# Attention feeding a gated MLP: token batches of 576 instead of chunks of 512, and weights that are loaded once and joined to float32 with a Prelu

## The chip, the cores and the metric

The kernel runs on one core of a Trainium2 chip. Its engines work in parallel, each on a queue of its own: TensorE (PE in the profile, its weight loads PEld), VectorE (DVE), ScalarE (ACT), GpSimd (POOL), and SyncE (SP), which issues the DMAs. The metric is the device time of one execution in microseconds (us), the median of several runs; lower is better.

## What is computed

Shapes: q, k, v are 8 batches x 8 heads x 576 tokens x 64, float32. The attention's output, as 4608 tokens of 512 numbers, is the input of a gated MLP of width 1536. The MLP's weights are 64-bit floats in memory.

```python
# two attentions, added; scale = 1/8, factor = 4
q_d, k_d, v_d = means of q, k, v over groups of 4 tokens          # 144 rows
out_up    = repeat(softmax(scale * q_d @ k_d.T) @ v_d, 4 rows each)
scores    = where(abs(i - j) < 4, scale * q @ k.T, -1e9)
out_local = softmax(scores) @ v
x = (out_up + out_local).transpose(0, 2, 1, 3).reshape(4608, 512)
# the gated MLP
gate = 1 / (1 + exp(-(x @ w_gate)))                               # 512 -> 1536
val  = x @ w_val
out  = (gate * val) @ w_out                                       # 1536 -> 512
```

## The kernel before

**Attention** comes in 32 units: a unit is one batch and one pair of heads (unit u is batch u // 4, pair u % 4). A unit is written as some 13 steps (`unit_steps`): sums of 4 tokens on POOL (`sum4`, L384/L386), local scores (s, L465), maximum, subtraction and exponential (L476 to L478), sums and division (L483 to L487), the downsampled scores and their softmax (sd, e; L508 to L528), transposes (at, adt), v, and last `av_local` (x), which multiplies with v, adds the downsampled part (od) and writes a quarter of the contraction rows of a token tile `xT`, as a high and a low float16 half (L594/L596).

**The MLP** takes tokens in 9 chunks of 512 (CH). Every product of the MLP is made of float16 halves in three matmuls (high x high, high x low, low x high; `product`, L391 to L395). For one of 12 slices of the width (fc) `moe_gate` issues 4 x 3 matmuls of 512 columns, then ScalarE takes the tanh (L622); `moe_val` does the same with w_val, then VectorE multiplies (L630), ScalarE writes the high half g (L638) and VectorE the low half (L639); `moe_out` adds that slice's share to four accumulators o0 to o3, 4 x 3 matmuls. Gate, val and the four accumulators have one bank of PSUM each (ps_o), the attention two (ps_a). A chunk crosses batches, so the scales of tanh and of the evictions come in up to two segments.

**The weights** are 36 pieces (12 each of gate g, val v, out o), 128 x 512 of 64-bit words, 512 KB each. All of them are loaded twice, through five stage buffers. In the first pass ("m") VectorE takes the absolute maximum of the high words (`wmax`, L153), and scales, powers of two, are made of the maxima by `wscale` (one transpose and one matmul each time). In the second pass ("c") `wconv` makes float32 of the 64-bit words: ScalarE scales the high words (L206), VectorE shifts them (L207), joins the low words by an or (L208), and puts the sign in (L209); then a gate or val piece is split by ScalarE (high, L215) and POOL (low, L216), an out piece by ScalarE and VectorE (`split`, L157/L158).

**The order** of the work is written by hand: a table T of positions, `wpos`, `gpos`, `opos`, `base` and `offset`, puts units, weight steps and the 12 slices of chunk 0 in one list up to position C1 = 56; from chunk 1 on the program writes gate, val and the former slice's out, with unit steps between them (`run_steps`). All engines take their queues in that order, as a scheduler inside the compiler places it. Chunk 1 needs tokens of batches 0 and 1, so units 0 to 7 stand ahead of it. Dummy matmuls (`awake`) stand between the first units' steps.

```python
a = raw.tile([P, WPC], I32, tag="wa", name=f"wr{k}{i}", bufs=3)
nc.scalar.activation(h.bitcast(F32), h.bitcast(F32), AF.Copy, scale=hc[:, j : j + 1])
nc.vector.tensor_scalar(out=a, in0=h, scalar1=3, scalar2=None, op0=ALU.logical_shift_left)
nc.vector.scalar_tensor_tensor(out=a, in0=l, scalar=29, in1=a, op0=ALU.logical_shift_right, op1=ALU.bitwise_or)
nc.vector.scalar_tensor_tensor(out=a, in0=h, scalar=SIGNBIT, in1=a, op0=ALU.bitwise_and, op1=ALU.bitwise_or)
```

Of the kernel before, what the change touches and what calls it, by code (L numbers as in the profile page):

```python
# [35 lines left out]
NCHUNK = NT // CH  # L36
NFC = DFF // P
# [7 lines left out]
NWT = 1 + 2 * NPC  # L45
NST = 5
# [12 lines left out]
def attention_moe(ctx, tc, qk, qkd, v, vd, wg, wv, wo, mask, out):  # L59
# [71 lines left out]
    names = {}  # L134

    def uniq(k):
        names[k] = names.get(k, 0) + 1
        return f"{k}{names[k]}"

    def pow2(dst, src):  # L140
# [22 lines left out]
    pw = cp.tile([P, NWT], F32, tag="pw", name="pw")  # L170
# [15 lines left out]
    def wmax(t, o):  # L186
        absmax(o, t[:, :, 1].bitcast(F32))
# [676 lines left out]
```

## Time and profile before

| | us |
|---|---|
| median of 3 runs | 1111.18 (1107.99 to 1111.2) |
| the profiled execution | 1110.07 |
| its span in the trace | 1108.3 |
| PE busy | 1062.2 (96%) |
| DVE busy | 547.4 (49%) |
| ACT busy | 444.1 (40%) |
| POOL busy | 364.6 (33%) |

The span runs from the first to the last instruction that the profiler recorded. PE's busy time contains the dummy matmuls and the time in which a slow clock stretches a matmul, so it is no measure of useful work by itself. An engine's share over the whole span mixes stages: about the first fifth of the span converts weights and computes the first two batches' attention, the rest is the steady sequence of gate, val and out.

### The profile page before, as it was taken

What the parts mean: (1) busy time and instruction counts of PE and PEld (TensorE: products, weight loads), DVE (VectorE), ACT (ScalarE), POOL (GpSimd) and SP (SyncE); (2) the same over time, 40 slices, a digit from 0 to 9 for tenths busy, and PEclk for the clock granted to TensorE, in tenths of its full rate; (3) what the DMA queues carried; (4) which work ended last, traced back from release to release, by engine and by line L of the source; (5) the groups of instructions that cost most, each with busy time, mean ns of one, the idle gap of its engine ahead of it and who ended that gap; (6) DMA issues with size and microseconds to landing.
All of it is one profiled execution on the core that took longest, in us unless ns stands there. A gap on an engine that the chain in (4) does not pass through costs nothing.

```text
span 1108.3 us, 17149 instructions
## 1 busy us (share of the span) xinstructions
PE 1062.2 (96%) x6831; PEld 554.8 (50%) x6831; DVE 547.4 (49%) x1038; ACT 444.1 (40%) x1048; POOL 364.6 (33%) x426
## 2 busy tenths in 40 slices
PE   8768878999998999999999999999999999999998
PEld 6543434655554555555555555555555544444443
DVE  5779989763445444444444444444444422212112
ACT  5535656443444443444334443444344422112112
POOL 8535755332433443333333443333332200000000
PEclk9859988999999999999999999999999999999999
DMA  9987866331213222232212221321120000000001
GB/s 361 382 313 262 275 211 210 110 118 59 70 56 136 70 71 70 71 109 71 70 57 101 74 80 59 109 71 59 59 97 1 2 1 38 1 1 38 1 1 38
DMA packets 31903, 110.38 MB, mean 100 GB/s; under 512 B 3536, under 2 KB 3664, under 8 KB 31824
## 3 DMA queue, kind: packets, MB, share of 16 engines
q1 hardware_dynamic: 31824, 109.30, 29.0%
q8 instruction: 54, 0.88, 0.3%
q14 instruction: 25, 0.20, 0.1%
HBM read 99.84 MB, written 9.44 MB: 99 GB/s over the span
## 4 chain that ended last, share of the span: by engine, by line
PE 86%; DVE 7%; POOL 2%; DMA 2%; ACT 2%; issue 1%; SPq 0%; DVEq 0%; POOLq 0%
PE po L395 25%; PE pv L395 24%; PE pg L395 23%; PE s L395 3%; PE x L395 3%; PE sd L395 3%; PE od L395 2%; PE at L543 2%; PE adt L553 1%; DMA qkd<-in_qkd_dram 1%; DVE hmx L153 1%; DVE wrv L209 1%; DVE wrg L208 1%; POOL kdblk L386 1%; DMA wg6c<-in_wg_dram 0%
## 5 line engine op out<-in xcount | busy, mean ns | idle before, releaser
L395 PE MATMUL pg<-xT,wg 128*128 128x512 f16 x1296 | 312.5, 383 | 11.2 <-ACT wg L215 7.3
L395 PE MATMUL pv<-xT,wv 128*128 128x512 f16 x1296 | 310.3, 381 | 5.3 <-DVE tanh L630 3.1
L395 PE MATMUL po<-g,wo 128*128 128x512 f16 x1188 | 281.2, 379 | 0.0
L395 PEld LDWEIGHTS <-wg 128*128 128x128 f16 x1296 | 125.3, 98 | 158.3 <-ACT wg L215 8.6
L395 PEld LDWEIGHTS <-wo 128*128 128x128 f16 x1296 | 126.4, 98 | 150.8 <-ACT wo L157 3.9
L395 PEld LDWEIGHTS <-wv 128*128 128x128 f16 x1296 | 125.6, 98 | 150.1 <-issue 6.4
L630 DVE SCALAR_TENSOR_TENSOR tanh<-tanh,pv 128x512 f32<-128x512 f32 x108 | 73.9, 684 | 210.2 <-PE pv L395 206.4
L622 ACT ACTIVATE tanh<-pg,tsc 128x512 f32<-128x512 f32 (+7 forms) x192 | 86.7, 497 | 176.4 <-PE pg L395 176.2
L638 ACT ACTIVATE g<-tanh,gs 128x512 f16<-128x512 f32 x99 | 71.4, 721 | 137.4 <-DVE tanh L630 135.6
L639 DVE SCALAR_TENSOR_TENSOR g<-tanh,gs,g 128x512 f16<-128x512 f32 x99 | 84.1, 849 | 52.9 <-ACT g L638 52.5
L477 POOL TENSOR_TENSOR t<-t,mx 128x640 f32<-128x640 f32 x32 | 43.4, 1357 | 164.0 <-DVE mx L476 160.1
L596 POOL TENSOR_TENSOR xT<-xs,xT 128x384 f16<-128x384 f32 (+7 forms) x54 | 48.5, 911 | 48.1 <-ACT xT L594 47.5
L585 DVE TENSOR_TENSOR xs<-x,od 128x464 f32<-128x464 f32 (+1 forms) x56 | 23.5, 452 | 72.3 <-PE x L395 72.3
L487 POOL TENSOR_TENSOR t<-t,sm 128x640 f32<-128x640 f32 x28 | 36.1, 1290 | 68.9 <-DVE sm L485 61.3
L465 DVE SCALAR_TENSOR_TENSOR t<-s,mk 128x384 f32<-128x384 f32 x64 | 30.8, 485 | 54.8 <-PE s L395 54.7
L157 ACT ACTIVATE vblk<-v,svb 64x640 f16<-64x640 f32 x48 | 39.6, 825 | 34.3 <-PE x L395 33.6
L395 PEld LDWEIGHTS s<-qk 64*64 64x64 f32 x1200 | 41.0, 138 | 21.5 <-issue 16.3
L158 DVE SCALAR_TENSOR_TENSOR vblk<-v,svb,vblk 64x640 f16<-64x640 f32 x48 | 47.9, 998 | 3.8 <-ACT vblk L157 1.7
L395 PE MATMUL s<-qk 64*64 64x64 f32 x1200 | 48.9, 227 | 0.6 <-ACT adt L535 0.6
L528 POOL TENSOR_TENSOR ad<-e,sme 72x288 f32<-72x288 f32 x52 | 37.1, 733 | 35.2 <-DVE sme L519 34.8
L511 ACT ACTIVATE e<-sd,mxd 72x144 f32<-72x144 f32 x128 | 47.1, 371 | 2.8
L384 POOL TENSOR_TENSOR qkd<-qkd 128x576 f32<-128x576 f32 x29 | 35.0, 1208 | 37.6 <-DMA qkd<-in_qkd_dram 36.9
(295 smaller groups left out, 1105.1 us busy)
## 6 DMA issues: line engine op xcount, KB each, us to landing
qk<-in_qk_dram SPq DMA_DIRECT2D x30, 610.0 KB, 3.9
qkd<-in_qkd_dram SPq DMA_DIRECT2D x29, 576.0 KB, 3.7
vd<-in_vd_dram SPq DMA_DIRECT2D x29, 384.0 KB, 3.1
v<-in_v_dram SPq DMA_DIRECT2D x32, 320.0 KB, 3.0
out_dram<-osb SPq DMA_DIRECT2D x16, 512.0 KB, 2.6
wo<-in_qk_dram SPq DMA_DIRECT2D x2, 610.0 KB, 9.9
wo<-in_qkd_dram SPq DMA_DIRECT2D x2, 576.0 KB, 9.5
out_dram<-osb SPq DMA_DIRECT2D x4, 256.0 KB, 2.4
```

Of the source, the lines that this page charges most:

```text
L157: nc.scalar.activation(hi, src, AF.Copy, scale=sc)
L158: nc.vector.scalar_tensor_tensor(out=lo, in0=src, scalar=sc, in1=hi, op0=ALU.mult, op1=ALU.subtract)
L395: nc.tensor.matmul(o, w[a], x[c], start=first and i == 0, stop=last and i == len(pairs) - 1)
L477: nc.gpsimd.tensor_tensor(out=t, in0=t, in1=mx.unsqueeze(2).to_broadcast([P, NBLK, WIN]), op=ALU.subtract)
L487: eng.tensor_tensor(out=t, in0=t, in1=sm.unsqueeze(2).to_broadcast([P, NBLK, WIN]), op=ALU.mult)
L511: nc.scalar.activation(s["e"][:, qb, h, :], pt[:QM, h * SD : (h + 1) * SD], AF.Exp, bias=mx[:, h : h + 1], scale=QKSCALE / 16, accum_out=s ...
L528: eng.tensor_tensor(out=AD[:, qb].rearrange("p c h k -> p h c k")[:, :, :, :KC], in0=s["e"][:, qb].rearrange("p h (c k) -> p h c k", c=NKC ...
L596: eng.tensor_tensor(out=x[:, hp, 1, o : o + n], in0=src, in1=x[:, hp, 0, o : o + n], op=ALU.subtract)
L622: nc.scalar.activation(t[:, o : o + n], pt[:, o : o + n], AF.Tanh, scale=tsc[:, b, fc : fc + 1])
L630: nc.vector.scalar_tensor_tensor(out=t, in0=t, scalar=1.0, in1=pt, op0=ALU.add, op1=ALU.mult)
L638: nc.scalar.activation(g[:, 0], t, AF.Copy, scale=gs[:, fc : fc + 1])
L639: nc.vector.scalar_tensor_tensor(out=g[:, 1], in0=t, scalar=gs[:, fc : fc + 1], in1=g[:, 0], op0=ALU.mult, op1=ALU.subtract)
```

## The change

- Tokens come by batches of 576 (8 of them) instead of chunks of 512 (9). Each gate, val or out tile is two halves of 288 columns (HN), each in a bank of its own, so a tile has two banks; gate, val, out and the dummy matmuls share one pool of two such tiles (ps_m), the attention has four banks. tanh, the product and g's halves take all 576 columns in one instruction each, with one scale per batch.
- `moe_out` no longer follows every slice: g of all 12 slices is kept (gq), and after a batch's last val four out tiles follow, 2 x 36 matmuls each.
- Each weight piece is loaded once, through four stage buffers. `wjoin` makes float32 of it at once: a Prelu on ScalarE with scale 2^-108 and alpha -2^32 leaves the sign where the shift keeps it, so the sign instruction goes; a shift and an or on VectorE follow, and the absolute maximum is taken of the joined numbers, which stay as float32 in place of the coming halves. Later, for two slices at a time (`wscale`) or for all out pieces (`oscale`), the scale is made, and `wsplit` splits: for gate and val VectorE multiplies by the scale in place (L249), ScalarE writes the high half and POOL the low half; for out ScalarE and VectorE split with the scale, as before.
- In each gate and val the contraction runs from the last quarter to the first, so the first matmul needs the batch's last unit.
- The order is a new table T; all loads are chained in the order in which they are written (`load`, `issue_after`).

VectorE, slices 3 and 4 of chunk 0, before: a stretch of its queue in the opening. wrv and wrg are the pieces in conversion, wv5c and wg5c their raw words, wo5m and wo6m out pieces in the first pass, t, s, sm, sme tiles of units.

```order
L207 TENSOR_SCALAR wrv5_1160<-wv5c_1101 128x512
L208 SCALAR_TENSOR_TENSOR wrg5_1122<-wg5c_1061,wrg5_1122 128x512
L153 TENSOR_REDUCE hmx_131<-wo5m_1103 128x1
L639 SCALAR_TENSOR_TENSOR wo16_111<-tanh_0_3_1196,gs_132,wo16_111 128x512
L518 TENSOR_SCALAR sme_5_1154<-sme_5_1154 72x4
L208 SCALAR_TENSOR_TENSOR wrv5_1160<-wv5c_1101,wrv5_1160 128x512
L153 TENSOR_REDUCE hmx_131<-wo6m_1167 128x1
L209 SCALAR_TENSOR_TENSOR wrg5_1122<-wg5c_1061,wrg5_1122 128x512
L465 SCALAR_TENSOR_TENSOR t_6_1310<-s_6_0_1297,mk_108 128x384
L519 RECIPROCAL sme_5_1154<-sme_5_1154 72x4
L209 SCALAR_TENSOR_TENSOR wrv5_1160<-wv5c_1101,wrv5_1160 128x512
```

The same engine after, at the first val of batch 0. The tiles wg16, wv16 hold the float32 in place of the halves, wg5 and wv5 are raw words, cw and ew scales.

```order
L249 TENSOR_SCALAR wg16_109<-wg16_109,cw_130 128x512
L249 TENSOR_SCALAR wv16_110<-wv16_110,cw_130 128x512
L208 TENSOR_SCALAR wg16_109<-wg5_917 128x512
L209 SCALAR_TENSOR_TENSOR wg16_109<-wg5_917,wg16_109 128x512
L159 TENSOR_REDUCE hmx_128<-wg16_109 128x1
L208 TENSOR_SCALAR wv16_110<-wv5_919 128x512
L209 SCALAR_TENSOR_TENSOR wv16_110<-wv5_919,wv16_110 128x512
L591 SCALAR_TENSOR_TENSOR tanh_0_0_847<-tanh_0_0_847,pv_0_0_868 128x576
L159 TENSOR_REDUCE hmx_128<-wv16_110 128x1
L164 SCALAR_TENSOR_TENSOR gq_112<-tanh_0_0_847,gq_112 128x576
```

A piece had three instructions (L207, L208, L209) and a maximum of another load; now it has a shift, an or and a maximum in a row, and a multiplication later (L249; four pieces in a row, of which the last two are shown).

ScalarE in the steady part, before (chunk 4, slices 4 and 5): tanh, the high half g, and steps of units 21 and 22 between them.

```order
L622 ACTIVATE tanh_4_4_6249<-pg_4_4_6236,tsc_139 128x256 x2
L535 COPY adt16_21_6017<-adt_21_6010 128x432
L509 ACTIVATE mxd_22_1_6021<-mxd_22_1_6021 72x2
L511 ACTIVATE e_22_5935,sme_22_5936<-sd_22_1_6019,mxd_22_1_6021 72x144 x2
L638 ACTIVATE g_4_4_6272<-tanh_4_4_6249,gs_132 128x512
L567 ACTIVATE od16_21_6072<-od_21_6068,sxb_138 128x144
L157 ACTIVATE vblk_124<-v22_5182,svb_137 64x10x64 x2
L594 CAST xT5_4768<-xs_21_6111 128x192
L594 CAST xT6_5849<-xs_21_6111 128x384
L622 ACTIVATE tanh_4_5_6325<-pg_4_5_6312,tsc_139 128x256 x2
L638 ACTIVATE g_4_5_6352<-tanh_4_5_6325,gs_132 128x512
```

ScalarE after (batch 3, slices 3 and 4), with steps of units 16 and 17 between.

```order
L586 ACTIVATE tanh_3_3_6064<-pg_3_3_6039,tsc_137 128x576
L532 ACTIVATE od16_16_6072<-od_16_6068,sxb_136 128x144
L163 ACTIVATE gq_112<-tanh_3_3_6064 128x576
L474 ACTIVATE mxd_17_1_6104<-mxd_17_1_6104 72x2
L163 ACTIVATE vblk_125<-v17_5548,svb_135 64x10x64 x2
L476 ACTIVATE e_17_6009,sme_17_6010<-sd_17_1_6102,mxd_17_1_6104 72x144 x2
L557 CAST xT4_6144<-xs_16_6134 128x576
L586 ACTIVATE tanh_3_4_6172<-pg_3_4_6147,tsc_137 128x576
L163 ACTIVATE gq_112<-tanh_3_4_6172 128x576
```

tanh is one instruction of 576 columns instead of two of 256, x goes to one token tile instead of two, and no out stands between a val and the next gate.

```diff
+HN = S // 2
-NST = 5
+NST = 4
-WGROUPS = [(0, 4), (4, NPC)]
+WGROUPS = [(0, 2), (2, 4), (4, 6), (6, 8), (8, 10), (10, NPC)]
+WUP = 2.0 ** 32
+WORDS = 2.0 ** -108
...
-    ps_o = ctx.enter_context(tc.tile_pool(name="ps_o", bufs=1, space=PSUM))
-    ps_a = ctx.enter_context(tc.tile_pool(name="ps_a", bufs=2, space=PSUM))
+    ps_m = ctx.enter_context(tc.tile_pool(name="ps_m", bufs=2, space=PSUM))
+    ps_a = ctx.enter_context(tc.tile_pool(name="ps_a", bufs=4, space=PSUM))
...
+    def load(dst_, src):
+
+        with tc.issue_after(last_load[0]) if last_load[0] is not None else nullcontext():
+            last_load[0] = nc.sync.dma_start(dst_, src).ins
...
+    def wjoin(k, i, after):
+
+        t = wraw.pop((k, i))
         h, l = t[:, :, 1], t[:, :, 0]
+        a = wwide(k, i).bitcast(I32)
+        nc.scalar.activation(h.bitcast(F32), h.bitcast(F32), AF.Prelu, scale=WORDS, alpha=-(2.0 ** 32))
+        with behind(after):
+            nc.vector.tensor_scalar(out=a, in0=h, scalar1=3, scalar2=None, op0=ALU.logical_shift_left)
+        nc.vector.scalar_tensor_tensor(out=a, in0=l, scalar=29, in1=a, op0=ALU.logical_shift_right, op1=ALU.bitwise_or)
+        j = 2 * NPC + i if k == "o" else 2 * i + (k == "v")
+        absmax(hmx[:, j : j + 1], wwide(k, i))
...
+    def wsplit(k, i):
+
+        a = wwide(k, i)
+        hi, lo = (home[k][:, wslot(k, i), e] for e in range(2))
+        sc = co[:, i : i + 1] if k == "o" else cw[:, i, "gv".index(k) : "gv".index(k) + 1]
+        if k == "o":
+            split(hi, lo, a, sc)
+        else:
+            nc.vector.tensor_scalar(out=a, in0=a, scalar1=sc, scalar2=None, op0=ALU.mult)
+            nc.scalar.copy(hi, a)
+            nc.gpsimd.tensor_tensor(out=lo, in0=a, in1=hi, op=ALU.subtract)
-        nc.scalar.activation(h.bitcast(F32), h.bitcast(F32), AF.Copy, scale=hc[:, j : j + 1])
-        nc.vector.tensor_scalar(out=a, in0=h, scalar1=3, scalar2=None, op0=ALU.logical_shift_left)
-        nc.vector.scalar_tensor_tensor(out=a, in0=l, scalar=29, in1=a, op0=ALU.logical_shift_right, op1=ALU.bitwise_or)
-        nc.vector.scalar_tensor_tensor(out=a, in0=h, scalar=SIGNBIT, in1=a, op0=ALU.bitwise_and, op1=ALU.bitwise_or)
...
+    def moe_in(b, w, x, k, fc, name):
+        pt = mm(name)
+        for h in range(2):
+            f = slice(h * HN, (h + 1) * HN)
+            for j in reversed(range(4)):
+                product(pt[:, h, :HN], [w[:, fc, a, j, :] for a in range(2)], [x[:, j, e, f] for e in range(2)], j == 3, j == 0)
+        return pt[:, :, :HN]
...
+    def moe_out(b, m):
+        pt = mm(f"po_{b}_{m}")
+        for h in range(2):
+            for n in range(NFC):
+                fc = n // 2 + NFC // 2 * (n % 2)
+                product(pt[:, h, :HN], [wo16[:, wslot("o", fc), a, m * P : (m + 1) * P] for a in range(2)],
+                        [gq[:, fc, e, h * HN : (h + 1) * HN] for e in range(2)], n == 0, n == NFC - 1)
```

## Rows read from the trace of the kernel before

**Rows 1.** Busy time by stretch: start:end, length, PE, PEld, DVE, ACT, POOL, clock, DMA, GB/s

```profile
0.00:68.90 68.90, 55.40 (x450) 42.09 (x450) 48.40 (x113) 33.38 (x96) 38.53 (x59) 0.81 0.94 357
68.90:73.50 4.60, 0.00 (x0) 0.00 (x0) 4.57 (x9) 3.04 (x8) 1.31 (x1) 0.50 1.00 391
73.50:214.00 140.50, 120.54 (x653) 59.91 (x654) 131.81 (x238) 81.44 (x161) 79.29 (x66) 0.90 0.68 228
...
214.00:1104.00 890.00, 886.22 (x5730) 452.77 (x5727) 362.39 (x680) 325.76 (x783) 245.51 (x300) 1.00 0.18 57
```

**Rows 2.** Chain of waits, 600 to 660 us: start, length, what

```profile
604.04 2.59 PE pg L395 x12
...
623.51 0.81 PE x L395 x30
```

**Rows 3.** Instructions that touch pg, pv and po, 214 to 1104 us, PE first

```profile
214.00:1104.00 890.00, 273.29 (x1152) 78.70 (x181) 1.00 0.18 57
...
214.00:1104.00 890.00, 275.27 (x1162) 66.43 (x97) 1.00 0.18 57
...
214.00:1104.00 890.00, 281.19 (x1188) 9.12 (x18) 20.54 (x46) 1.00 0.18 57
```

**Rows 4.** What DVE waited for, 73.5 to 214 us: total, times, longest

```profile
DVE tanh L630 <- PE pv L395: 3.4, 3, 1.8
DVE wo L639 <- ACT wo L638: 3.1, 1, 3.1
```

**Rows 5.** DVE's instructions in order of time, 109 to 116 us: start, duration

```profile
108.72 0.73 DVE L639 SCALAR_TENSOR_TENSOR wo<-tanh,gs,wo 128x512 f16<-128x512 f32 x1
109.38 0.68 DVE L208 SCALAR_TENSOR_TENSOR wrv<-wv4c,wrv 128x512 int32<-128x512 int32 x1
109.98 0.67 DVE L153 TENSOR_REDUCE hmx<-wo4m 128x1 f32<-128x512 f32 x1
110.58 0.53 DVE L484 TENSOR_SCALAR sm<-sm 128x10 f32<-128x10 f32 x1
...
111.09 0.67 DVE L630 SCALAR_TENSOR_TENSOR tanh<-tanh,pv 128x512 f32<-128x512 f32 x1
111.68 0.44 DVE L508 TENSOR_REDUCE mxd<-sd 72x2 f32<-72x288 f32 x1
112.05 0.41 DVE L207 TENSOR_SCALAR wrg<-wg5c 128x512 int32<-128x512 int32 x1
112.38 0.68 DVE L209 SCALAR_TENSOR_TENSOR wrv<-wv4c,wrv 128x512 int32<-128x512 int32 x1
112.98 0.20 DVE L485 RECIPROCAL sm<-sm 128x10 f32<-128x10 f32 x1
```

**Rows 6.** DVE busy by line, 73.5 to 214 us: L207, L208, L209, L153

```profile
73.50:214.00 140.50, 17.74 (x34) 0.90 0.68 228
...
73.50:214.00 140.50, 28.68 (x35) 0.90 0.68 228
...
73.50:214.00 140.50, 30.49 (x35) 0.90 0.68 228
...
73.50:214.00 140.50, 14.75 (x21) 0.90 0.68 228
```

**Rows 7.** DVE groups by form, 0 to 214 us: busy, mean ns, idle before

```profile
L208 DVE SCALAR_TENSOR_TENSOR wrv<-wv10c,wrv 128x512 int32<-128x512 int32 x1 | 1.7, 1744 | 0.0
...
L207 DVE TENSOR_SCALAR wrg<-wg10c 128x512 int32<-128x512 int32 x1 | 1.5, 1470 | 1.0 <-POOL wg L216 1.0
```

**Rows 8.** PE's instructions, 72 to 78 us; in brackets idle before, its releaser

```profile
73.53 1.03 PE L395 MATMUL pg<-xT,wg 128*128 128x512 f16 x2 [4.95 <-ACT wg L215]
```

**Rows 9.** Chain of waits, 1090 to 1109 us

```profile
1098.55 5.19 PE po L395 x24
```

**Rows 10.** Chain of waits, 338 to 362 us

```profile
345.55 3.43 DMA vd<-in_vd_dram
```

**Rows 11.** Costliest groups of the page: busy, mean ns, idle before and releaser

```profile
L622 ACT ACTIVATE tanh<-pg,tsc 128x512 f32<-128x512 f32 (+7 forms) x192 | 86.7, 497 | 176.4 <-PE pg L395 176.2
```

More of the change, by code (lines that the diff above doesn't have):

```diff
@@ L73, in awake @@
     def awake(n):
-        pt = ps_o.tile([P, 512], F32, tag="val", name="awake")
+        pt = mm("awake")
         for i in range(n):
-            nc.tensor.matmul(pt[:, :256], idle[:, :P], idle, start=True, stop=True)
-    awake(T["k0"])
+            nc.tensor.matmul(pt[:, 0, :256], idle[:, :P], idle, start=True, stop=True)
+    awake(30)
     ident = cp.tile([P, P], F32, tag="ident", name="ident")
@@ L397, in attention_moe @@
     owner = {}
-    done = set()
     def own(t, u):
@@ new lines, in attention_moe, with moe_gate @@
+    tg = {}
+    def moe_in(b, w, x, k, fc, name):
+        assert (k, fc) in done and all(u in done for u in range(b * NPAIR, (b + 1) * NPAIR)), (b, k, fc)
+        pt = mm(name)
[4 more added lines that the diff above has]
+        return pt[:, :, :HN]
+    def moe_gate(b, fc):
+        pt = moe_in(b, wg16, xT[b], "g", fc, f"pg_{b}_{fc}")
+        t = tg[b, fc] = wk.tile([P, 2, HN], F32, tag="tanh", name=f"tanh_{b}_{fc}")
+        nc.scalar.activation(t, pt, AF.Tanh, scale=tsc[:, b, fc : fc + 1])
@@ new lines, in moe_val @@
+    def moe_val(b, fc):
+        pt = moe_in(b, wv16, xT[b], "v", fc, f"pv_{b}_{fc}")
+        t = tg.pop((b, fc))
+        nc.vector.scalar_tensor_tensor(out=t, in0=t, scalar=1.0, in1=pt, op0=ALU.add, op1=ALU.mult)
+        mark["g", b, fc] = split(*[gq[:, fc, e].rearrange("p (h c) -> p h c", h=2) for e in range(2)], t, GSC).ins
+    def moe_out(b, m):
+        assert all(("o", i) in done for i in range(NPC))
+        pt = mm(f"po_{b}_{m}")
[4 more added lines that the diff above has]
+                        [gq[:, fc, e, h * HN : (h + 1) * HN] for e in range(2)], n == 0, n == NFC - 1)
+        osb = raw.tile([P, 2 * WPC], F32, tag="stage", name=f"osb{b}_{m}", bufs=NST)[:, :S].rearrange("p (h c) -> p h c", h=2)
+        last = b == B - 1 and m == 3
+        for h in [slice(0, 1), slice(1, 2)] if last else [slice(0, 2)]:
+            if m % 2 and not (last and h.start == 0):
+                nc.vector.tensor_scalar(out=osb[:, h], in0=pt[:, h, :HN], scalar1=osc[:, b : b + 1], scalar2=None, op0=ALU.mult)
+            else:
+                nc.scalar.activation(osb[:, h], pt[:, h, :HN], AF.Copy, scale=osc[:, b : b + 1])
+        osb = osb.rearrange("p h c -> p (h c)")
+        for c, o, i, n in segs_of_batch(b):
+            nc.sync.dma_start(out[c, m // 2][:, m % 2, o : o + n], osb[:, i : i + n])
@@ L791, in _layout @@
+    for p in sorted(steps):
+        for f in steps[p]:
+            f()
 def _layout(q, k, v, wg, wv, wo):
```

501 lines of the change are left out of this document (186 added, 315 removed).

## Prediction

> **What bounds the kernel now.** First the table of four stretches [rows 1]. From 214 us to 1104 us TensorE is busy 886.22 of 890.00 us at the full clock, and no other engine is above 453: here the kernel is as long as its matmuls. Before 214 us it is not: TensorE is busy 175.94 us by the three rows above (55.40 + 0.00 + 120.54), part of that dummy matmuls that only keep it awake, and VectorE (DVE) is the busy one: 131.81 of 140.50 us between 73.5 and 214, with the first MoE matmul at 73.53 [rows 8]. The second view is what VectorE waits for in that stretch [rows 4]: 3.4 and 3.1 us are the largest entries of 8.4 in all, so from 73.5 to 214 us it simply has too much work, and TensorE stands waiting behind it. So I cost two things apart: the matmul stream (a price per matmul) and the opening (a list of VectorE work).
>
> **The matmul stream.** The chain of waits gives twelve 512-column matmuls in 2.59 us, 215.8 ns each: 512 columns at 2.4 GHz are 213.3, so 2.5 ns lie over that. Thirty 58-column matmuls, each with a weight load of its own, take 0.81 us, 27.0 ns each: 24.2 and 2.8 [rows 2]. A 288-column matmul was not run before; between those two it should take 120.0 + 2.5 = 122.5 ns (122.8 at the other end). Before, 9 chunks x 432 = 3888 matmuls x 0.2158 = 839.0 us; after, 8 batches x 864 = 6912 x 0.1225 = 846.7 us. **The smaller column count costs +7.7 us** (bounds: 0 if the overhead did not recur, +9.8 with 2.8 ns).
>
> That stretch as a model: 1152 gate, 1162 val and 1188 out matmuls started in it [rows 3], 3502 x 0.2158 = 755.7 us; the remaining 134.3 of 890.0 are the attention of 24 units (5.6 us each) with every stall. Two DMA waits are among those: one of 3.43 us for vd stands on the chain near 346 us [rows 10]. After, the stretch from batch 1 on holds 7 x 864 = 6048 matmuls = 740.9 us and the same 24 units. I carry the 134.3, less 1.5 for scores of unit 8 that stand ahead of batch 1, less 2 (half of what I hold the DMA waits to be worth: the loads are chained in order now, which may remove or move them) = 130.8. The last 24 matmuls ended at 1098.55 + 5.19 = 1103.74 [rows 9], so the tail was 4.5 us; the last tile is now evicted in two halves by two engines as before, so 4.5 again. **From the first gate of batch 1 to the end: 740.9 + 130.8 + 4.5 = 876 us.** What the 12% larger tiles make of tanh and the evictions lies beside TensorE.
>
> **The opening, to the first gate of batch 1.** Per weight piece VectorE used to run a shift, an or and a sign instruction, and an absmax in the first pass: 0.52, 0.82, 0.87 and 0.70 us mean (17.74/34, 28.68/35, 30.49/35, 14.75/21; [rows 6]). Started one behind the other they go faster than their records: the shift to the next start 0.33, the or 0.60, the absmax 0.60, the sign 0.60, tanh times val 0.59, the lo half 0.66 [rows 5]. Removed: 36 sign instructions, 21.6 us at that pace and 31.4 at the means. Added: 24 multiplications by a scale (gate and val pieces only). No such instruction is in the trace; the nearest is the shift, one input from SBUF, one scalar, the same 128x512: 0.33 to 0.52, and 1.47 for one that coincided with a POOL instruction [rows 7]. I take 0.4: 9.6 us, bounds 8 and 35. VectorE's net is thus -12 to -22, at worst +14. ScalarE's scaling becomes a Prelu, one for one, and I cost that at nothing (ScalarE is busy 81.44 of 140.50 [rows 1]; if a Prelu took 0.3 us longer, 36 of them would be 11 us, against 59 idle). Loading each piece once removes 18.9 MB; DMA was busy at 0.94 and 1.00 before 73.5 us but at 0.68 after [rows 1], so this can pay only ahead of the first gate.
>
> The multiplications and the two other instructions share buffers with POOL's lo subtraction. [Rows 7] show a shift of 1.47 us and an or of 1.74, against 0.41 and 0.68 in [rows 5]: something held them for about a microsecond. The Trainium skill ("SBUF — State Buffer", "Who interferes with whom") says that VectorE in its two-port modes, which a tensor_scalar can enter, and GpSimd lock each other out for a whole instruction; this speaks against adding 24 tensor_scalars next to 24 POOL subtractions. The stretched rows agree with it in kind, though not every shift that ran beside POOL is long. Were all 24 held as that shift was, 24 x 1.07 = 26 us would come on top of the 9.6, which is the upper bound above.
>
> Now stage by stage. *(a) To the first gate.* Before 73.5, of which 4.95 were a wait for the first gate piece's cast [rows 8]. After, the first two pairs of pieces are in the first loads, and the queue holds 109 VectorE instructions up to the last xT of batch 0, some 49 us of work as against 48.40 + 4.57 before [rows 1]; all four units of batch 0 must be done first, since the matmuls start with the last quarter of the contraction. I take **64** (bounds 56 if the DMA is no longer the pace, 73.5 if nothing is won). *(b) Gates and vals of batch 0.* VectorE's queue from there to the last gq holds 28 joins (16 gate and val pieces, 12 out pieces), 20 multiplications, 12 tanh times val, 12 lo halves, five groups of scales, and parts of units 4 and 5. At the pace: 28 x (0.33 + 0.60 + 0.60) = 42.8; 20 x 0.33 = 6.6; 12 x (0.59 + 0.66) x 576/512 = 16.9; scales some 6 and units some 10: 82 us. At the means of [rows 6] it is 28 x 2.04 = 57.1 and 20 x 0.52 = 10.4: 100. TensorE's own 24 x 12 x 2 x 0.1225 = 70.6 fits below. I take 88 and 6% idle as between 73.5 and 214: **94** (82 to 106). *(c) Out of batch 0 with units 4 to 7.* Out can begin only when all 12 out pieces are scaled together. TensorE: 288 x 0.1225 = 35.3, four units x 5.6 = 22, and some 4 for the scale's way through two transposes: **61** (57 to 70). Here VectorE has 12 splits and the rest of four units, less than that. The clock was 0.90 of full between 73.5 and 214 us, where TensorE waited, and 1.00 after [rows 1]; in (b) VectorE sets the pace and a slower TensorE is covered (70.6 / 0.90 = 78), in (c) TensorE is busy and I take the full clock.
>
> **Sum.** First gate of batch 1 at 64 + 94 + 61 = 219 (bounds 195 to 245); end at 219 + 876 = 1095 of span. The profiled run took 1110.07 with a span of 1108.3, so 1.8 lie around it: **1097 us**. Against 1110.07 that is -13, and the median of the runs, 1111.18, is 0.1% above the profiled run, which I leave out. In other words: before, 214 us held the opening and 386 matmuls (83 us) of the MoE; after, 219 hold it with all 864 matmuls of batch 0 (106 us), and 8 us come back as shorter matmuls.
>
> **The rivals.** *Faster opening.* If VectorE keeps the pace of [rows 5] throughout and DMA relief brings the first gate to 58: 58 + 82 + 57 = 197, and **1075**. For it: one instruction less in a queue 94% full. Against: the means of [rows 6] lie well above the pace.
> *PSUM handover (slower).* Gate, val and out now take turns in two buffers. Before, a gate's buffer was wanted again after a val and an out, 2 x 2.59 us; now after one val, 24 x 0.1225 = 2.94 us, in which ScalarE must read the whole tile: a tanh of 576 columns (86.7 us for 108 tiles, 0.80 each, [rows 11]; about the same for 576 columns in one piece). That leaves 2.1 us for ScalarE or VectorE to be late, and both have queues of unit work; 176.2 of the 176.4 us of ScalarE's idle time ahead of tanh end with the gate, so tanh mostly waits for TensorE and not the reverse. It decides from a mean loss of 0.11 us at each of 168 gate and val handovers of batches 1 to 7: 19 us, **1116**.
> *Late opening (slower).* Out of batch 0 no longer overlaps its gates: if the joins run at the means and the multiplications are held as in [rows 7], (b) is 106 + 20, T is 64 + 126 + 57 = 247, and **1125**. For it: [rows 7], and two of the three instructions of a join are of that kind. Against: before, more of the same instructions, with the signs and units 4 to 7, fitted into 140.5 us.
> *It does not reach the bound.* If ahead of 214 us the pace is set by units and loads and not by the weight work, the 12 to 22 us are eaten: T about 235, **1112**, no change.
> *The price of a matmul.* A longer step per 288-column matmul at any floor, say 0.15 us, would cost 6912 x 0.0275 = +190 us, **1287**. The 27.0 ns of [rows 2], weight load included, exclude a floor in this program. The Trainium skill ("TensorE: Matmul & The Clock Gate", "Back-to-back issue gap") gives sustained weight-and-matmul pairs at 81 ns for 128 columns and 131 for 512, by which 288 would take an estimated 102 and the change would cost nearly 200 us; the 215.8 and 27.0 ns contradict both ends.
>
> **How the numbers follow.** Forecast 0.60 (1075 to 1107), faster opening 0.15, handover 0.08, late opening 0.08, no reach 0.07, price of a matmul 0.02. Runs of this kernel tell 0.3% from no change, that is 1107.8 to 1114.5. Faster 0.75; same 0.09 (no reach and the mild end of the handover); slower 0.16. The range leaves out a tenth below (half of the faster opening) and a tenth above: 1070 to 1117.
>
> **What would show it.** Right: the first gate near 64, the last val of batch 0 near 158, the first gate of batch 1 near 219, twelve 288-column matmuls in 1.47 us, and TensorE nearly unbroken from there. Wrong: waits of gate or val matmuls for tanh (handover); multiplications of over a microsecond (late opening); a first gate of batch 1 before 200 or after 240; or 876 us for the rest missed by more than 10.

## The result, and the profile after

The changed kernel takes 1093.46 us (median of 4 runs, 1091.73 to 1095.66) against 1111.19 before: ratio 0.9848, 95% interval 0.9826 to 0.987, 17.7 us faster. The forecast was 1097 within 1070 to 1117. The profiled run, the slowest of the four, took 1095.66 with a span of 1093.9, 14.4 us less than the profiled run before (1110.07); all stages below are of that run.

| us | forecast | after |
|---|---|---|
| (a) to the first gate | 64 | 66.7 |
| (b) gates and vals of batch 0 | 94 | 95.5 |
| (c) out of batch 0, to the first gate of batch 1 | 61 | 65.5 |
| first gate of batch 1 | 219 | 227.7 |
| from there to the end of the span | 876 | 866.2 |
| span | 1095 | 1093.9 |

The stages, as busy time of PE, PEld, DVE, ACT and POOL, then the clock, the DMA share and GB/s; these answer to [rows 1]:

```profile
0.00:66.70 66.70, 56.20 (x479) 47.31 (x480) 46.32 (x109) 39.99 (x105) 34.53 (x47) 0.79 0.59 214
66.70:162.20 95.50, 84.09 (x678) 62.67 (x677) 88.10 (x178) 46.85 (x86) 47.21 (x37) 0.95 0.57 196
162.20:227.70 65.50, 60.75 (x577) 49.17 (x576) 41.25 (x85) 29.75 (x73) 34.08 (x37) 1.00 0.34 114
227.70:1089.70 862.00, 862.00 (x8206) 693.37 (x8204) 339.51 (x640) 276.28 (x613) 229.66 (x274) 1.00 0.18 59
```

What to see: the second row is the stage in which VectorE is full again (88.10 of 95.50), as it was in the third line of [rows 1]; in the last row TensorE does not stand for a moment. PE's instructions at the two borders (start, duration; in brackets the idle time ahead and what ended it):

```profile
173.24 0.66 PE L365 MATMUL po<-gq,wo 128*128 128x288 f16 x4 [1.78 <-ACT wo L163]
...
227.66 1.51 PE L365 MATMUL pg<-xT,wg 128*128 128x288 f16 x11
```

And the chain of waits in the steady part and at the end, which answers to [rows 2] and [rows 9] (start, length, what):

```profile
406.81 0.37 PE pv L365 x3
...
411.82 0.92 PE x L365 x30
...
416.40 2.94 PE pv L365 x24
...
1079.92 9.81 PE po L365 x80
```

24 matmuls in 2.94 us and 80 in 9.81 are 122.5 and 122.6 ns for 288 columns.

**Where the time went, before against after.** The border that answers to the first gate of batch 1 is, before, the first gate of chunk 1, which started at 228.1 us (its first matmuls, then the busy times from there to the last matmul):

```profile
228.13 2.12 PE L395 MATMUL pg<-xT,wg 128*128 128x512 f16 x9
...
228.10:1103.70 875.60, 872.09 (x5622) 444.27 (x5618) 357.15 (x671) 322.23 (x776) 242.51 (x296) 1.00 0.18 57
```

So the opening did not become shorter (228.1 to 227.7); it does more in the same time, namely the whole MLP of 576 tokens instead of 512. From the border to the last matmul it was 1103.7 - 228.1 = 875.6 and is 862.0. Of those 13.6 us, 4.9 are matmuls of the MLP (3456 x 0.2158 = 745.8 before, 6048 x 0.1225 = 740.9 after), and 8.7 are what stood between them: 129.8 before, 121.1 now, for the same 24 units. Of these 8.7, 3.5 are time in which TensorE stood (875.60 - 872.09; the waits of [rows 10] and their like); after 227.7 us no PE wait is left in the trace. The other 5.2 lie inside TensorE's busy time. About 1 of them is four matmuls of a unit (sd) that now stand ahead of the border; where the rest went was not shown.

### The profile page after: what moved, and what is told of

Same layout as the page of the kernel before. It is cut to its first block, busy times and chain, and to the rows that moved or that the text cites. A ratio compares the mean times of both kernels' runs of the same rounds, so it can differ in the third digit from the quotient of the medians.

```text
span 1093.9 us, 23031 instructions
## 1 busy us (share of the span) xinstructions
PE 1063.1 (97%) x9935; PEld 852.5 (78%) x9935; DVE 515.7 (47%) x1010; ACT 393.4 (36%) x878; POOL 345.5 (32%) x395
## 4 chain that ended last, share of the span: by engine, by line
PE 86%; DVE 6%; POOL 2%; ACT 2%; DMA 2%; issue 1%; SPq 0%; ACTq 0%; DVEq 0%; POOLq 0%
PE po L365 25%; PE pg L365 23%; PE pv L365 23%; PE s L365 3%; PE x L365 3%; PE sd L365 2%; PE od L365 2%; PE at L508 1%; DMA wv<-in_wv_dram 1%; PE adt L518 1%; PE awake L82 1%; POOL wg L251 1%; DMA wg<-in_wg_dram 1%; DVE wv L209 1%; DVE hmx L159 1%
## 5 line engine op out<-in xcount | busy, mean ns | idle before, releaser
L365 PE MATMUL pg<-xT,wg 128*128 128x288 f16 x2304 | 304.7, 289 | 8.6 <-POOL wg L251 5.7
L365 PE MATMUL pv<-xT,wv 128*128 128x288 f16 x2304 | 301.8, 286 | 2.5 <-DVE tanh L591 2.4
L365 PE MATMUL po<-gq,wo 128*128 128x288 f16 x2304 | 289.4, 286 | 2.9 <-ACT wo L163 1.8
L365 PEld LDWEIGHTS <-wg 128*128 128x128 f16 x2304 | 224.5, 99 | 71.4 <-POOL wg L251 6.6
L365 PEld LDWEIGHTS <-wo 128*128 128x128 f16 x2304 | 223.3, 98 | 61.1 <-ACT wo L163 2.6
L365 PEld LDWEIGHTS <-wv 128*128 128x128 f16 x2304 | 224.0, 98 | 59.1 <-issue 3.1
L591 DVE SCALAR_TENSOR_TENSOR tanh<-tanh,pv 128x576 f32<-128x576 f32 x96 | 72.0, 750 | 203.3 <-PE pv L365 203.2
L163 ACT ACTIVATE gq<-tanh 128x576 f16<-128x576 f32 x96 | 65.6, 684 | 200.5 <-DVE tanh L591 199.8
L586 ACT ACTIVATE tanh<-pg,tsc 128x576 f32<-128x576 f32 x96 | 70.9, 739 | 123.7 <-PE pg L365 123.7
L164 DVE SCALAR_TENSOR_TENSOR gq<-tanh,gq 128x576 f16<-128x576 f32 x96 | 79.1, 824 | 25.9 <-ACT gq L163 25.4
L606 DVE TENSOR_SCALAR osb<-po,osc 128x576 f32<-128x576 f32 (+1 forms) x16 | 12.8, 799 | 125.1 <-PE po L365 107.8
L164 DVE SCALAR_TENSOR_TENSOR vblk<-v,svb,vblk 64x640 f16<-64x640 f32 x48 | 46.3, 965 | 5.1 <-ACT vblk L163 4.3
```

Of the source, the lines that this page charges most:

```text
L164: return nc.vector.scalar_tensor_tensor(out=lo, in0=src, scalar=sc, in1=hi, op0=ALU.mult, op1=ALU.subtract)
L365: nc.tensor.matmul(o, w[a], x[c], start=first and i == 0, stop=last and i == len(pairs) - 1)
L586: nc.scalar.activation(t, pt, AF.Tanh, scale=tsc[:, b, fc : fc + 1])
L591: nc.vector.scalar_tensor_tensor(out=t, in0=t, scalar=1.0, in1=pt, op0=ALU.add, op1=ALU.mult)
```

## The experiments

Each is one edit to the changed kernel, unless it says "before". Medians are of 4 runs each (6 for six stage buffers); ratios are to the kernel before on the same chip, whose medians were 1111.2 to 1111.5. The stages of an experiment come from one trace. The traces of the changed kernel and of experiments 4 and 6 show how much they differ by themselves, since the engines run the same instructions in the same order there up to 158 us: the first gate came at 66.7, 67.4 and 62.8 us, and stage (b) took 95.5, 97.8 and 97.5. A difference as small as these shows nothing.

**1. The Prelu undone.**

```diff
-nc.scalar.activation(h.bitcast(F32), h.bitcast(F32), AF.Prelu, scale=WORDS, alpha=-(2.0 ** 32))
+nc.scalar.activation(h.bitcast(F32), h.bitcast(F32), AF.Copy, scale=WORDS)
...
+nc.vector.scalar_tensor_tensor(out=a, in0=h, scalar=SIGNBIT, in1=a, op0=ALU.bitwise_and, op1=ALU.bitwise_or)
```

> The changed kernel with its Prelu undone: ScalarE copies with the scale 2^-108, and the sign instruction on VectorE is back for each of the 36 pieces. Theory 1 (VectorE's queue paces the opening): 32 of the 36 stand ahead of the last val of batch 0, each 0.60 us at VectorE's pace to 0.87 at the mean of before, so +19 to +28 us, 1112 to 1121; the last val moves from 162 to 180 or later. Theory 2 (loads and POOL pace it, VectorE's idle time takes the signs): +0 to +6, at most 1100.

1118.71 us, ratio 1.0063 (1.0045 to 1.0081): 25 us slower than with the Prelu, and slower than before the change, as theory 1 said. Busy time by stage, and then the sign line (L210) alone on VectorE:

```profile
67.90:182.70 114.80, 89.26 (x678) 64.32 (x678) 111.13 (x211) 47.23 (x86) 46.44 (x38) 0.87 0.48 163
182.70:249.80 67.10, 63.00 (x577) 51.87 (x576) 41.99 (x80) 30.18 (x73) 35.05 (x37) 0.95 0.32 112
249.80:1112.00 862.20, 862.05 (x8206) 693.37 (x8204) 338.93 (x640) 276.21 (x614) 230.38 (x274) 1.00 0.18 59
...
67.90:182.70 114.80, 23.40 (x28) 0.87 0.48 163
```

Stage (b) grew from 95.5 to 114.8 us, by 19.3, and VectorE's busy time in it from 88.10 to 111.13, by 23.0, of which the 28 signs are 23.40. What is added to VectorE's queue there comes out at the end almost in full (the two profiled runs are 22.1 us apart); loads and POOL did not absorb it. The rest is untouched (862.0 and 862.2). ScalarE's Prelu took 0.672 to 0.682 us (medians of the three kinds of pieces) and the plain copy that replaced it 0.667 to 0.676, so the sign costs next to nothing there:

```profile
L206 ACT ACTIVATE wg<-wg x12: 653/672/697, 18.8 to 114.7; 128x512 f32<-128x512 f32 x12
```

```profile
L207 ACT ACTIVATE wg<-wg x12: 647/667/688, 18.6 to 127.8; 128x512 f32<-128x512 f32 x12
```

(The first row is of the changed kernel, the second of the one with the Prelu undone: durations in ns, lowest, median, highest.)

**2. The Prelu alone, in the kernel before.**

```diff
-nc.scalar.activation(h.bitcast(F32), h.bitcast(F32), AF.Copy, scale=hc[:, j : j + 1])
+nc.scalar.activation(h.bitcast(F32), h.bitcast(F32), AF.Prelu, scale=hc[:, j : j + 1], alpha=-(2.0 ** 32))
...
-nc.vector.scalar_tensor_tensor(out=a, in0=h, scalar=SIGNBIT, in1=a, op0=ALU.bitwise_and, op1=ALU.bitwise_or)
```

> The kernel before with this one part of the change: ScalarE scales the high words with a Prelu of alpha -2^32, and the sign instruction of the 36 pieces is gone; loads, chunks and order as before. Theory 1 (VectorE paces the opening): 36 x 0.60 to 0.87 = 22 to 31 us of VectorE's work less in a stretch 94% full, of which perhaps two thirds reach the end: -14 to -22, 1089 to 1097, so most of the gain of the whole change. Theory 2 (the gain came from loading once and from the batches): 0 to -5, 1106 to 1111.

1096.44 us, ratio 0.9863 (0.9845 to 0.988). The two-line edit alone cannot be told from the whole change: the intervals of the two ratios overlap. This is theory 1. The busy times from the first gate to 202.7 us, then from the first gate of chunk 1 to the last matmul:

```profile
73.10:202.70 129.60, 115.92 (x661) 58.63 (x662) 114.39 (x203) 81.19 (x161) 71.56 (x66) 0.96 0.72 250
...
215.20:1090.00 874.80, 871.85 (x5620) 444.31 (x5618) 359.33 (x671) 321.70 (x776) 242.16 (x296) 1.00 0.17 57
```

The first gate comes at 73.1 as before, the first gate of chunk 1 at 215.2 instead of 228.1, the rest stays at 874.8. The four kernels make a table:

| us | sign on VectorE | sign by the Prelu |
|---|---|---|
| chunks of 512, loaded twice | 1111.5 | 1096.4 |
| batches of 576, loaded once | 1118.7 | 1093.5 |

So the batches and the single load, taken together, cost 7 us with the old sign. With the new one they gain 3, which is within the noise. The profiled runs show why it matters which sign they come with. Behind the border they save about the same with both: 13.4 us with the old sign (875.6 to 862.2), 12.8 with the new one (874.8 to 862.0). The opening grows with both, but by 21.7 us with the old sign (228.1 to 249.8) and by 12.5 with the new one (215.2 to 227.7). Batches and single load were not undone apart from each other.

**3. The multiplications on ScalarE.**

```diff
-nc.vector.tensor_scalar(out=a, in0=a, scalar1=sc, scalar2=None, op0=ALU.mult)
+nc.scalar.activation(a, a, AF.Copy, scale=sc)
```

> The changed kernel with the 24 multiplications of gate and val pieces by their scale moved from VectorE to ScalarE. Theory 1 (VectorE paces the gates of batch 0): 20 of them, 0.40 us each at its pace, leave the stretch from 67 to 162 us: -5 to -8, 1085 to 1089. Theory 2 (the chain there runs over loads and POOL's subtractions, and ScalarE's 0.7 us come instead of 0.4 in each piece's way): -1 to +4.

1101.61 us, ratio 0.9902 (0.9879 to 0.9925): 8 us slower, beyond what either theory gave. Stage (b), whole, with the same multiplications gone from VectorE (8.52 us for 20 in the changed kernel); then the shift (L208) and the low halves (L164) there, first here, then in the changed kernel:

```profile
68.80:170.50 101.70, 86.95 (x679) 63.86 (x680) 90.08 (x171) 58.67 (x106) 43.17 (x38) 0.92 0.52 184
...
68.80:170.40 101.60, 17.91 (x28) 0.92 0.52 184
...
68.80:170.40 101.60, 13.66 (x12) 0.92 0.52 184
```

```profile
66.70:162.10 95.40, 14.41 (x28) 0.95 0.57 196
...
66.70:162.10 95.40, 10.50 (x12) 0.95 0.57 196
```

VectorE's busy time did not fall: 88.1 to 90.1 us with seven instructions fewer (20 are gone, 13 others fall into the longer stage). The same 28 shifts and 12 low halves took 6.7 us longer, and waits for ScalarE rose. So VectorE's busy time is not a fixed sum of work: it contains time for which an instruction is held. One such shift, and what POOL ran then:

```profile
131.29 1.42 DVE L208 TENSOR_SCALAR wv<-wv 128x512 int32<-128x512 int32 x1
...
131.26 1.16 POOL L251 TENSOR_TENSOR wg<-wg 128x512 f16<-128x512 f32 x1 [9.92 <-ACT wg L250]
```

In this stage 16 VectorE instructions take over 0.6 us more than the median of their kind, together 13.9 us more; in the changed kernel 8 do, together 6.6 us more. Every one of the 24 began while POOL ran an instruction. That points to POOL as what holds them, though no run slowed or sped up POOL. Part of the difference belongs to the single trace: in those of experiments 4 and 6, with the changed kernel's order, it is 12 instructions and 10.6 us, and 13 and 10.8.

**4. The scale of the out pieces on ScalarE.** On the chain of the changed kernel, behind the last val of batch 0, stood one 12-column VectorE instruction of 3.88 us; POOL ran five instructions in a row over that time:

```profile
167.82 0.81 DVE L441 TENSOR_REDUCE mx<-t 128x10 f32<-128x640 f32 x1
168.55 3.88 DVE L234 TENSOR_SCALAR co<-ew,rv,so 128x12 f32<-128x12 f32 x1
172.34 0.44 DVE L473 TENSOR_REDUCE mxd<-sd 72x2 f32<-72x288 f32 x1
```

```profile
168.00 1.29 POOL L493 TENSOR_TENSOR ad<-e,sme 72x288 f32<-72x288 f32 x2 [2.10 <-DVE so L152]
169.25 1.26 POOL L442 TENSOR_TENSOR t<-t,mx 128x640 f32<-128x640 f32 x1
170.47 1.14 POOL L354 TENSOR_TENSOR qkd<-qkd 128x576 f32<-128x576 f32 x1
171.57 0.82 POOL L354 TENSOR_TENSOR vd<-vd 128x384 f32<-128x384 f32 x1
```

```diff
-nc.vector.tensor_scalar(out=co, in0=ew[:, :, 1], scalar1=rv, scalar2=so, op0=ALU.mult, op1=ALU.mult)
+nc.scalar.activation(co, ew[:, :, 1], AF.Copy, scale=rv)
+nc.scalar.activation(co, co, AF.Copy, scale=so)
```

> The changed kernel with the one 12-column scale of the out pieces (3.88 us on VectorE in the trace of after, beside four POOL instructions in a row) made by two small ScalarE instructions instead. Theory 1 (VectorE was held by POOL there, and out of batch 0 waited for it): the scale takes under 0.6 us and the first out matmul comes some 3 us sooner: -2 to -4. Theory 2 (the 12 splits that follow set the pace): no change, within 1 us.

1096.48 us, ratio 0.9859 (0.9827 to 0.989), not to be told from the changed kernel. The two instructions took 0.31 us each, and the first out matmul came 9.2 us after the last val matmul instead of 11.1; but stage (c) as a whole was 66.2 us against 65.5, and the out matmuls then waited 2.8 us for the low halves of the out pieces (0.9 in the changed kernel). The hold itself did not go away. It fell on VectorE's first low half of an out piece, beside the same POOL instructions:

```profile
172.26 3.61 DVE L164 SCALAR_TENSOR_TENSOR wo<-wo,co 128x512 f16<-128x512 f32 x1
...
172.18 1.25 POOL L443 TENSOR_TENSOR t<-t,mx 128x640 f32<-128x640 f32 x1
173.40 1.14 POOL L355 TENSOR_TENSOR qkd<-qkd 128x576 f32<-128x576 f32 x1
174.50 0.82 POOL L355 TENSOR_TENSOR vd<-vd 128x384 f32<-128x384 f32 x1
```

In the changed kernel such a low half takes 0.77 us in the median. So it was not the 12 columns that were slow: in both traces the VectorE instruction that met this row of POOL instructions was held until vd was done. In both traces POOL went on at once with its next instruction (kdblk, at 172.36 in the changed kernel); why the hold ended there is not shown.

**5. Keeping TensorE awake in the opening.** Between 40 and 68 us TensorE's clock was 0.50 of full (1.2 GHz) in the changed kernel; TensorE had stood from 38.2 us on, until 45.0.

```diff
+add(T["p1x"] + 0.01, lambda: awake(60))
+add(T["p2od"] - 0.01, lambda: awake(6))
+add(T["p3od"] - 0.01, lambda: awake(6))
```

> The changed kernel with 72 more dummy matmuls of 256 columns ahead of the matmuls of units 2 and 3, 60 of them behind x of unit 1, where TensorE stands from 38 to 45 us and its clock falls to half until 69 us. Theory 1 (the units' matmuls at half clock stand on the chain to the first gate: x, od, at and adt of two units, some 16 us at half clock): first gate 6 to 8 us sooner, and the same at the end, 1085 to 1088. Theory 2 (the joins of batch 0 go on during that time and then pace the gates whenever the first one starts): first gate sooner, last val of batch 0 less than 3 us sooner, 1090 to 1094.

1099.87 us, ratio 0.989 (0.9865 to 0.9915), 6 us slower (runs from 1096.12 to 1105.16, the profiled one the slowest); a miss for both theories. The first gate came at 72.2, not at 60. The clock held until 48 us and then fell all the same:

```profile
44.00:48.00 4.00, 2.41 (x21) 1.73 (x18) 4.00 (x9) 2.27 (x4) 0.00 (x0) 1.00 0.76 229
48.00:52.00 4.00, 2.51 (x8) 1.68 (x9) 3.81 (x10) 3.54 (x11) 0.00 (x0) 0.68 0.62 193
...
60.00:64.00 4.00, 4.00 (x22) 3.65 (x21) 2.05 (x7) 1.55 (x3) 0.00 (x0) 0.50 0.00 0
```

and the extra work changed the order in which the compiler's scheduler placed the queues: ScalarE now took two weight pieces whose loads had not landed ahead of a softmax of units 2 and 3 (chain of waits):

```profile
42.09 4.13 DMA wo<-in_wo_dram
...
49.94 4.04 DMA wv<-in_wv_dram
...
54.75 0.72 ACT e L476 x4
```

What the half clock costs by itself is therefore not settled by this run. The trace of experiment 6 says something of it: its edit touches batches 1 to 7 only, its order is that of the changed kernel, but TensorE had nearly the full clock between 48 and 52 us (changed kernel first, then experiment 6):

```profile
48.00:52.00 4.00, 3.07 (x15) 2.42 (x14) 1.56 (x4) 3.20 (x12) 0.00 (x0) 0.50 0.49 160
```

```profile
48.00:52.00 4.00, 3.10 (x28) 2.91 (x28) 1.21 (x4) 3.52 (x15) 0.00 (x0) 0.99 0.32 116
```

TensorE was 0.9 us ahead of the changed kernel at 46.6 us and 3.9 ahead at 59.4, and so was the first gate (62.8 instead of 66.7); the last val was only 1.9 ahead (160.2) and the first gate of batch 1 1.8 (225.9). That is what theory 2 said, from one pair of traces; why the clock was higher there is not shown.

**6. The handover of PSUM buffers.**

```diff
 nc.scalar.activation(t, pt, AF.Tanh, scale=tsc[:, b, fc : fc + 1])
+if b > 0:
+    nc.scalar.activation(t, pt, AF.Tanh, scale=tsc[:, b, fc : fc + 1])
```

> The changed kernel with the tanh of every gate tile of batches 1 to 7 taken twice, so that each of the 84 gate buffers comes free 0.74 us later. Handover rival of the prediction (a mean loss of 0.11 us per handover is near): +19 us or more, 1112 and above. My theory (2.94 us for one buffer, of which tanh takes 0.74, leaves enough): +0 to +4, at most 1098, and no waits of gate, val or out matmuls for tanh.

1096.78 us, ratio 0.9876 (0.9841 to 0.9911). From the first gate of batch 1 to the last matmul TensorE is still unbroken, with 62.1 us more on ScalarE:

```profile
225.85:1089.44 863.59, 863.59 (x8206) 693.75 (x8204) 340.51 (x640) 335.81 (x697) 229.08 (x274) 1.00 0.18 59
...
L588 ACT ACTIVATE tanh<-pg,tsc 128x576 f32<-128x576 f32 x84 | 62.1, 739 | 2.3
```

(The second row is the page's form of a group: busy us, mean ns, idle before.) A buffer that comes free 0.74 us later costs 1.5 us in this part (862.1 in the changed kernel, from the start of its first gate), where 84 x 0.74 would be 62: two buffers have that much room, and the handover rival is out. The median is 3.3 us over the changed kernel's, within the noise of these runs (1092.81 to 1101.82).

**7. Three stage buffers, and the second load back.**

```diff
-NST = 4
+NST = 3
...
-for n, prev in zip(order[NST:], order):
+for n, prev in zip(order[NST + 1:], order[1:]):
```

> The changed kernel with three stage buffers for the weights instead of four, the loads of pieces following the joins by three. Theory 1 (VectorE's queue paces the gates of batch 0): a piece's cycle of load, Prelu, shift and or is short against three pieces' share of the stretch (95 us for 28 pieces, 3.4 us each), +0 to +5, at most 1099. Theory 2 (the refill of a stage buffer, load 3.5 to 5 us and two engines' queues, is the pace beside VectorE): the stretch grows by a tenth or more, +10 to +30.

1102.95 us, ratio 0.993 (0.991 to 0.9951), 9 us slower, just short of theory 2; stage (b) grew by a tenth, from 95.5 to 104.9 us. With three buffers loaded twice:

```diff
+twin = raw.tile([P, WPC, 2], I32, tag="twin", name=f"w{k}{i}twin", bufs=1)
+load(twin.rearrange("p a b -> p (a b)"), srcs[k][i].bitcast(I32))
 load(t.rearrange("p a b -> p (a b)"), srcs[k][i].bitcast(I32))
```

> As the one with three stage buffers, but each weight piece is loaded twice, first into a tile that nobody reads, so that the 18.9 MB are back. If the bytes of the second loading were a cost by themselves: +10 or more over three stage buffers alone. By my theory (DMA busy at 0.57 between 67 and 162 us; only the refill's latency grows by some 1.4 us): +0 to +6 over it.

1116.12 us, ratio 1.005 (1.003 to 1.0071): 13 us over three buffers alone, more than I expected. Stage (b) of the two, in that order:

```profile
67.10:172.00 104.90, 85.58 (x678) 63.23 (x678) 95.28 (x189) 48.30 (x87) 46.26 (x38) 0.91 0.54 183
```

```profile
65.40:174.70 109.30, 88.32 (x672) 63.63 (x671) 90.54 (x172) 46.06 (x81) 37.11 (x32) 0.88 0.80 279
```

VectorE is busy 95.28 of 104.90 us in the first and 90.54 of 109.30 in the second, where its waits for the Prelu of a piece add up to 15.9 us. So the second loads do cost with three buffers, though the DMA engines are busy only 0.80. In the profiled runs 4.4 us of the cost lie in stage (b) and 7.6 in stage (c) (65.1 to 72.7), of which the account above explains only the first; the first gate came 1.7 earlier. All loads are chained, and the second ones go into one tile, so the run does not tell their bytes from their place in the chain. With four buffers, or with the five of the kernel before, it was not tried.

**8. Six stage buffers, without and with the multiplications on ScalarE.**

```diff
+if n % NSLOT < NST:
+    t = raw.tile([P, WPC, 2], I32, tag="stage", name=f"w{k}{i}", bufs=NST)
+else:
+    xtile(0)
+    room1 = xtile(1).rearrange("p a e s -> p (a e s)").bitcast(I32)
+    o = (n % NSLOT - NST) * 2 * WPC
+    t = room1[:, o : o + 2 * WPC].rearrange("p (a b) -> p a b", b=2)
```

> The changed kernel with six stage buffers for the weights: two more lie in the second xT tile, which is empty until unit 4 writes it, and a piece's load follows the join six before it. Three buffers instead of four cost +9.4 us between the first gate and the last val of batch 0. Theory 1 (the refill of a buffer is a pace of that stretch beside VectorE): it falls from 95 us towards VectorE's own work of 82 to 88, -5 to -10 at the end, 1084 to 1089. Theory 2 (with four buffers VectorE alone is the pace, and only three were too few): within 2 us, 1092 to 1096.

1101.23 us, ratio 0.9918 (0.9901 to 0.9934), 8 us slower; the profiled run (1099.34) is 3.7 over that of the changed kernel, so the trace shows only half of it.

```profile
70.40:168.30 97.90, 87.98 (x679) 64.66 (x679) 92.34 (x190) 45.63 (x84) 46.33 (x38) 0.91 0.51 180
```

Six buffers do not shorten stage (b), 97.9 against 95.5 us, with VectorE busy 92.34: four are enough, as theory 2 said of that stage. And they move joins ahead of unit 3 in the queues; the first gate comes at 70.4 instead of 66.7.

> As with six stage buffers, and the 24 multiplications moved from VectorE to ScalarE besides, which alone cost +8 us with four buffers. Theory 1 (that loss came from the refill, which ScalarE's longer queue delayed): now a gain of 3 to 8 us over six buffers alone. Theory 2 (it came from VectorE's instructions being held longer by POOL, since they meet it more often): again 0 to +8 over six buffers alone.

1097.03 us, ratio 0.9874 (0.986 to 0.9887): 4 us better than six buffers alone, as theory 1 said, and no better than the changed kernel. Stage (b) is 94.8 us here, although 12 VectorE instructions take together 11.2 us over their medians, more than with six buffers alone (7 and 6.5 us). That speaks for ScalarE's longer queue behind four buffers as a part, at least, of the loss of experiment 3.

None of the ten is faster than the changed kernel.

## Why the prediction was right, and where it was not

*What bounds.* Right: a full VectorE queue in the opening, TensorE afterwards. Experiments 1 and 2 show it from both sides: 36 signs back cost 25 us, 36 signs gone from before give 15. The signs named in the forecast came too: 66.7 for 64, 162.2 for 158, 227.7 for 219, TensorE unbroken from there.

*The price of a 288-column matmul.* 122.5 forecast, 122.5 and 122.6 measured, with a new weight load for each. The rival "price of a matmul" is out. The rule of the Trainium skill ("TensorE: Matmul & The Clock Gate", "Back-to-back issue gap") by which 288 columns would take an estimated 102 ns does not hold here.

*The multiplication.* 0.4 us forecast; four in a row start 0.39, 0.40 and 0.40 apart, the longest of the 24 took 0.68, and 20 of them were busy 8.52 us. The late-opening rival, in which POOL held them all, did not come.

```profile
70.64 0.48 DVE L249 TENSOR_SCALAR wg<-wg,cw 128x512 f32<-128x512 f32 x1
71.03 0.48 DVE L249 TENSOR_SCALAR wv<-wv,cw 128x512 f32<-128x512 f32 x1
71.43 0.48 DVE L249 TENSOR_SCALAR wg<-wg,cw 128x512 f32<-128x512 f32 x1
71.83 0.48 DVE L249 TENSOR_SCALAR wv<-wv,cw 128x512 f32<-128x512 f32 x1
```

*Stages (a) and (b).* 64 and 94 forecast, 66.7 and 95.5 measured. In (b) VectorE was busy 88.10 us, 92%, where 88 and 94% were assumed. That it met the 88 so closely is luck: it was chosen between 82 at the pace and 100 at the means, and the traces of experiments 4 and 6 have the same order and a (b) 2 us longer. (The 82 counts a multiplication at 0.33 us, not at the 0.4 of its price.)

*Stage (c), a term mis-sized.* 61 forecast, 65.5 measured: 35.3 of out as forecast, 25.4 instead of 22 for the rest of TensorE's work, and 4.8 instead of 4 in which it stood (65.5 - 60.75). The term that failed is the unit at 5.6 us, taken from units 8 to 31. Units 4 to 7 multiply with v in float32, the later ones in float16, and a float32 matmul of 58 columns took over three times as long (the 80 in stage (c), then those behind the border; busy us, mean ns, idle before):

```profile
L365 PE MATMUL x<-at,vblk 128*128 128x58 f32 x80 | 9.8, 269 | 0.0
...
L365 PE MATMUL x<-at,vblk 128*128 128x58 f16 x720 | 23.5, 189 | 0.0
```

By busy time that is 122 ns each against 33, some 7 us for the 80. Without it the 22 would have been too much, since parts of these units had already run in (b). The scale's way was priced about right: from the last val to the first out matmul it is 173.24 - 162.2 = 11.0 us, but other work on TensorE covers 7.4 of them. The held 12-column instruction lies in it, and experiment 4 shows that the low halves behind it would have been held in its place.

*The rest, mis-sized the other way.* 876 forecast, 866.2 measured, just within the 10 that the prediction allowed itself. The matmuls of the MLP were right to the microsecond; 130.8 us were carried for units and stalls, and it was 121.1. Of those 9.7 us, 3.0 were never part of this stretch: the 134.3 were counted from 214 us, and ahead of the border at 228.1 stood, besides the 1.5 of scores taken off, two pieces of unit 7:

```profile
215.80 0.90 PE L395 MATMUL od<-adt,vdblk 128*128 128x144 f32 x6
...
219.12 2.34 PE L395 MATMUL x<-at,vblk 128*128 128x58 f32 x20
```

Another 1.5 are waits: 2 were taken off for them, and all 3.5 went. The remaining 5.2 are the busy time of which the result's section could place only about 1. The two errors, +8.7 at the border and -9.8 behind it, cancel; that the total came nearer than its parts is luck. (The upper bound of the border is added up wrongly: 73.5 + 106 + 70 are 249.5, not 245. Nothing else uses it.)

*The loads.* The prediction let the 18.9 MB pay only ahead of the first gate. With three buffers that is wrong: in experiment 7 the second loads cost 13 us, all of it behind the first gate. What they cost with the five buffers of the kernel before is open.

*The bounds of "VectorE paces".* The prediction treated stage (b) as a sum of VectorE's work. Adding to it does cost what it weighs (experiment 1: 19.3 us for 23.4). Taking away 8.5 us did not give them back (experiment 3), since other instructions were then held for longer and ScalarE's queue grew. So such a sum tells what added work costs better than what work taken away gives back.

*What the change is worth by parts.* The forecast did not split its -13 by parts; measured, the Prelu gains 15 us in the kernel before and 25 in the changed one, and batches with the single load lose 7 without it and gain 3, within the noise, with it.

## What to carry to other kernels

When one engine's queue is full, look for an instruction on it that another engine can do inside one that it runs anyway: the sign by a Prelu cost ScalarE next to nothing and, by itself, gave as much as the whole change. Undo each part alone before crediting a large change, in both kernels: the table of four told here that the restructuring loses without the Prelu, and with it gains no more than the noise. Take the price of a piece of work from the stage that it will run in: a unit of the opening was not a unit of the steady part. Where a scheduler inside the compiler places the queues, an edit can move other work too: three edits here that were meant to relieve something (multiplications off VectorE, a clock kept up, two more buffers) lost 6 to 8 us, and in the last two the order of other work had changed.

## What the runs showed of the hardware

A VectorE instruction of 12 columns was held 3.88 us while POOL ran five instructions back to back, and ended 0.04 us after the last of them, 171.57 + 0.82 = 172.39; on ScalarE the same work took 2 x 0.31, and then another VectorE instruction was held 3.61 us in its place (experiment 4). The Trainium skill ("SBUF — State Buffer", "Who interferes with whom") says that VectorE in its two-port modes and GpSimd lock each other out for a whole instruction. This trace agrees in kind, and adds that a wait can last over several POOL instructions that follow each other without a gap.

TensorE ran 8206 instructions from 227.7 to 1089.7 us without a gap at the full clock. Matmuls of 288 columns took 122.5 ns there and those of 512 took 215.8 before, each 2.5 ns over its columns at 2.4 GHz, with a weight load for each.
